# Adding products into spectral sums by accumulating DMAs from GpSimd, and one more down projection by seven products, in a two-layer convolution and FFN kernel

## The chip, the core and the metric

The kernel runs on one core of one Trainium2 chip. The metric is device time in microseconds, from the start to the end of the program. Five engines work side by side: TensorE (PE, matmuls), VectorE (DVE), ScalarE (ACT), GpSimd (POOL) and SyncE (SP, which issues most DMAs). They meet at semaphores alone. Sixteen DMA engines move the data that any of them orders.

## The reference

Sequence length S = 2048, width D = 512, inner width F = 1792, everything bfloat16 outside. Two rounds of the same two layers:

```python
def _A_ref(q, k, v, shift_k, ssm_k, ssm_D):
    # k_shift: causal convolution of k with 4 taps
    kv = k_shift * v
    # y: convolution along S of kv with ssm_k, by FFTs of length 2 S
    y = y + kv * ssm_D[None, None, :]
    return q * y

def _B_ref(x, w_gate, w_up, w_down):
    g = _silu(x @ w_gate)
    u = x @ w_up
    return (g * u) @ w_down

x = A_q
x = x + _A_ref(_layernorm(x, axis=-1), A_k, A_v, A_shift_k, A_ssm_k, A_ssm_D)
x = x + _B_ref(_layernorm(x, axis=-1), B_w_gate, B_w_up, B_w_down)
x = x + _A_ref(_layernorm(x, axis=-1), A_k, A_v, A_shift_k, A_ssm_k, A_ssm_D)
x = x + _B_ref(_layernorm(x, axis=-1), B_w_gate, B_w_up, B_w_down)
```

The long convolution y depends on k, v and ssm_k alone, so both rounds use the same y.

## The kernel before

The sequence is cut into 4 blocks of 512 tokens (index c or b). Each block of 512 rows is a tile of 128 partitions by 4 rows by 512 columns. A unit (layer, c, h) is half a block, 256 tokens, in one FFN layer: 16 units in all, run in the order (0,c,0), (0,c,1), (1,c,0), (1,c,1) for c = 0 to 3.

**The convolution by blocks.** Each block of kv and of ssm_k is turned into a spectrum by matmuls with a table of cosines and sines (`fwd`), evacuated by ACT, and combined by sums and differences on DVE (`butterfly4`). X[i] is the spectrum of block i of kv, G[j] that of a pair of neighbouring blocks of the kernel. Output block k needs the sum Z[k] of all products X[i] G[j] with i + j = k. `product` makes one: two multiplications of 128x4096 elements into t1 and t2 (L765), and two sums or differences of 128x2048 elements (L769). The first product of a sum writes Z itself. Each later one leaves its result in t1, and a DVE addition of 128x4096 elements adds t1 to Z (L773). There are six of these: one into Z[1], two into Z[2], three into Z[3]. `inverse` then folds Z by half sums and differences (m<-Z, L653), some more sums into Z (L659, L670) and goes back by matmuls with the table `inv` (ps<-Z,inv), which ACT evacuates into Yk.

**The FFN of a unit.** `prologue` normalises the rows, multiplies by y, adds to x, normalises again (the z rows, L976 on DVE or L971 on ACT), and turns z into zT by DMA transposes from SP (L1006); the first unit alone is turned by PE (ptz<-ident,z, L1034). The statistics come from DVE (`ln_stats`, BN_STATS L926 and BN_AGGR L927) or from ACT (`ln_stats_act`, L941 and L950), and the reciprocal square root (rstd) from a small operation on POOL (L912), for which the normalising instructions wait. The tables ST1 and ST2 say which units use ACT. Then come the gate and up projections in four groups of 4, 4, 4 and 2 tiles of 128 columns of F: either with the weights standing (`ffn`, L1256) or row by row (`by_rows`), where the products hr<-hr,sg (L1204, L1201) are turned back into sg by two DMA transposes from SP (L1206). The down projection reads them: 14 tiles times 2 row groups of matmuls with 512 columns (pd, L1287).

**Seven products.** For the units in STRASSEN the down projection of some or all groups is done by `seven`: a 2 by 2 blocking of tokens, tiles of F and columns of D, with seven products of 256 columns for a pair of tiles in place of eight. Its left sides are sums of the gated tiles, made by three DVE instructions a group (cb, L1076, L1078, L1080), its right sides five sums of w_down made once (`weight_sums`, L1061). `add_seven` evacuates four banks on ACT (mt, L1109) and merges them into x by five DVE instructions (L1114 to L1121). Without it two evacuations (dn) and one DVE addition (L1339) do this.

**What sets the order.** All instructions are recorded first, with their buffers. ORDER, a table of numbers, gives each recorded operation its place, and the engines' queues are filled in that order. The planner's `walk` goes through the order with cost constants, gives out the buffers of each ring (the ring "s8" has 11 slots for spectra, "ht" 7 for FFN tiles, "pf" 4 banks of PSUM), and sets where filler matmuls go at the start. Each engine works its queue strictly in order.

Of the kernel before, what the change touches and what calls it, by code (L numbers as in the profile page):

```python
# [9 lines left out]
P = 128  # L10
# [11 lines left out]
ST2 = lambda l, c, h: (l, c, h) in {(0, 0, 0), (0, 2, 1), (1, 2, 1)}  # L22
K_ACT = lambda b: b in {2, 3}
PW = 0.7
# [6 lines left out]
STRASSEN={(1,2,1):4,(0,3,0):4,(0,3,1):4,(1,3,0):4,(1,3,1):2}  # L31
# [125 lines left out]
class Plan:  # L157
# [15 lines left out]
    def add(self, eng, cost, emit, r=(), w=(), lat=None, due=None, conv=False, slack=0.0, after=(), dest=None):  # L173
# [22 lines left out]
        if o.late and any(q.eng == "ACT" for q in o.preds):  # L196
            o.late = 4
        if eng == "SP":
            o.late = 2 if cost == 1.29 else 3 if cost < 1 else 0
        o.count = 0  # L200
        if eng == "PE":
            o.count = 16
            for n in (512, 256, 128):
# [1402 lines left out]
```

## Time and profile before

| what | value |
| --- | --- |
| median of 3 runs | 338.25 us |
| lowest and highest run | 338.14 and 338.88 us |
| span of the profiled execution | 337.1 us |
| TensorE busy | 332.4 us, 2300 matmuls |
| VectorE busy | 314.3 us, 566 instructions |
| ScalarE busy | 269.4 us, 550 instructions |
| GpSimd busy | 36.1 us, 48 instructions |
| DMA, of all 16 engines' span | 38.3% in the queue of the kernel's own transfers |

The profile is of one execution; its own time is given as the span, from the first to the last instruction, and the runs' times lie about 1 us above it. Busy time of an engine counts instructions that overlap once. A matmul's end is modelled, so a busy TensorE may still have small holes between the starts of its matmuls. In a row of a group, the numbers behind the bar are the group's busy time and the mean of one instruction in ns, then the idle time just before them with what ended it. A row of the waits has the waiting instruction, what it waited for, the total in us, how many times, and the longest.

### The profile page before, as it was taken

How to read it: one execution, taken by the hardware profiler on the slowest of the kernel's cores; microseconds unless marked ns; L12 is line 12 of the kernel's file. 1: busy time of each engine (PE TensorE's matmuls, PEld its weight loads, DVE VectorE, ACT ScalarE, POOL GpSimd, SP SyncE). 2: the span in 40 equal slices, each digit the busy share in tenths (PEclk: the TensorE clock that was granted, in tenths of full speed). 3: DMA queues.
4: the chain of work that ended last, by engine and by line, in shares of the span. 5: the costliest groups of instructions: out<-in, count | busy, mean ns of one | idle time of the engine just before them, and what ended most of it. 6: DMA issues, size and time to landing. Idle time of an engine off the chain costs nothing.

```text
span 337.1 us, 6249 instructions
## 1 busy us (share of the span) xinstructions
PE 332.4 (99%) x2300; PEld 208.0 (62%) x2300; DVE 314.3 (93%) x566; ACT 269.4 (80%) x550; POOL 36.1 (11%) x48
## 2 busy tenths in 40 slices
PE   9999999999999999999999999999999999999996
PEld 7665865645445564644545474654445787878994
DVE  7799999999999999999999999997898998986995
ACT  6999999999966684989999794989765748476862
POOL 4010100031210100022110200021000000000000
PEclk9999999999999999999999999999999999999999
DMA  7999403632354446253314433320415320203001
GB/s 278 331 281 387 65 3 77 140 93 34 78 94 86 95 88 146 72 80 74 69 33 83 104 81 102 81 53 10 84 33 95 65 65 16 42 8 64 2 33 62
DMA packets 75817, 31.08 MB, mean 92 GB/s; under 512 B 67589, under 2 KB 73610, under 8 KB 75786
## 3 DMA queue, kind: packets, MB, share of 16 engines
q1 hardware_dynamic: 75632, 30.61, 38.3%
q8 instruction: 18, 0.29, 0.4%
q14 instruction: 13, 0.11, 0.1%
q10 hardware_dynamic: 154, 0.07, 0.1%
HBM read 12.33 MB, written 2.10 MB: 43 GB/s over the span
## 4 chain that ended last, share of the span: by engine, by line
PE 85%; DVE 10%; ACT 2%; issue 1%; POOL 0%; POOLq 0%
PE pf L423 48%; PE pd L1287 19%; PE ps L1097 7%; PE ps L423 6%; PE pf L1171 4%; DVE t L755 1%; PE wm L1572 1%; DVE Z L759 1%; DVE bst L926 1%; DVE t L769 1%; ACT jk L950 1%; DVE Z L773 1%; DVE t L765 1%; DVE m L896 1%; DVE z L976 1%
## 5 line engine op out<-in xcount | busy, mean ns | idle before, releaser
L423 PEld LDWEIGHTS <-zT 128*128 128x128 bf16 x496 | 48.5, 98 | 55.1 <-issue 0.2
L423 PE MATMUL pf<-wu_sb,zT 128*128 128x512 bf16 x248 | 61.5, 379 | 0.0
L423 PE MATMUL pf<-wg_sb,zT 128*128 128x512 bf16 x248 | 61.4, 379 | 0.0
L423 PE MATMUL pf<-zT,wg_sb 128*128 128x256 bf16 x400 | 50.7, 273 | 0.3 <-DVE zT L1037 0.3
L1197 ACT ACTIVATE sg<-pf 128x512 bf16<-128x512 f32 x62 | 37.4, 615 | 14.9 <-PE pf L423 10.7
L1287 PE MATMUL pd<-wd_sb,sg 128*128 128x512 bf16 x200 | 48.9, 379 | 0.0
L1198 ACT CAST hr<-pf 128x512 bf16<-128x512 f32 x62 | 36.3, 599 | 12.7 <-PE pf L423 10.9
L423 PEld LDWEIGHTS <-wg_sb 128*128 128x128 bf16 x400 | 38.6, 98 | 8.3 <-issue 0.7
L765 DVE TENSOR_TENSOR t<-X,G 128x4096 bf16<-128x4096 bf16 x18 | 41.0, 2287 | 0.1
L1258 ACT ACTIVATE sg<-pf 128x512 bf16<-128x512 f32 x50 | 29.6, 603 | 7.7 <-PE pf L423 6.3
L423 PE MATMUL pf<-zT,wu_sb 128*128 128x256 bf16 x272 | 34.9, 273 | 0.1
L912 POOL TENSOR_TENSOR rstd<-mv,nhalf 128x2 f32<-128x2 f32 x20 | 18.3, 919 | 147.8 <-DVE mv L927 147.8
L1287 PEld LDWEIGHTS <-sg 128*128 128x128 bf16 x200 | 19.6, 98 | 21.4
L423 PEld LDWEIGHTS <-wu_sb 128*128 128x128 bf16 x272 | 26.5, 98 | 6.6 <-issue 0.4
L1287 PE MATMUL pd<-wd_sb,ht 128*128 128x512 bf16 (+1 forms) x126 | 29.6, 369 | 0.0
L912 POOL TENSOR_TENSOR rstd<-ve,nhalf 128x2 f32<-128x2 f32 x12 | 13.8, 1150 | 119.6 <-ACT ve L954 119.6
L926 DVE BATCH_NORM_STATS2 bst<-xc 128x6 f32<-128x512 bf16 x40 | 26.3, 685 | 0.3
L1262 ACT CAST ht<-pf 128x512 bf16<-128x512 f32 x34 | 20.2, 599 | 1.6 <-PE pf L423 1.5
L1287 PEld LDWEIGHTS <-ht 128*128 128x128 bf16 x126 | 12.3, 98 | 13.4 <-DVE ht L1267 0.4
L532 ACT ACTIVATE X<-ps 128x512 bf16<-128x512 f32 x32 | 18.6, 606 | 2.3 <-PE ps L423 1.6
L1267 DVE TENSOR_TENSOR ht<-ht,sg 128x1024 bf16<-128x1024 bf16 (+1 forms) x33 | 18.3, 556 | 0.7 <-ACT sg L1258 0.4
L1204 DVE TENSOR_TENSOR hr<-hr,sg 128x1024 bf16<-128x1024 bf16 x25 | 17.1, 683 | 1.3 <-ACT sg L1197 0.9
(157 smaller groups left out, 590.9 us busy)
## 6 DMA issues: line engine op xcount, KB each, us to landing
hn<-in_A_ssm_k_dram SPq DMA_DIRECT2D x4, 512.0 KB, 4.0
vt<-in_A_v_dram SPq DMA_DIRECT2D x4, 512.0 KB, 6.0
xc<-in_A_q_dram SPq DMA_DIRECT2D x4, 512.0 KB, 5.3
out_dram<-xc SPq DMA_DIRECT2D x15, 128.0 KB, 1.9
wg_sb<-in_B_w_gate_dram SPq DMA_DIRECT2D x1, 1792.0 KB
wu_sb<-in_B_w_up_dram SPq DMA_DIRECT2D x1, 1792.0 KB, 7.6
wd_sb<-in_B_w_down_dram SPq DMA_DIRECT2D x1, 1280.0 KB, 11.5
sg<-hr SPq DMA_TRANSPOSE x62, 2.4
```

The lines of the kernel that those rows point to most:

```text
L423: nc.tensor.matmul(o, lhsT=lhsT, rhs=rhs, start=(n == 0), stop=(n == len(terms) - 1))
L532: add("ACT", act(D), lambda: nc.scalar.activation(out=view(), in_=ps.t[:], func=ACT.Copy, scale=scale), r=[ps], w=[(buf, keys)], conv=conv)
L765: dve(8 * D, lambda t=t, part=part: nc.vector.tensor_mul(out=t.t[:], in0=x.t[:, :, part:part + 1, :].to_broadcast((P, R, 2, D)), in1=g.t[: ...
L912: add("POOL", cost, lambda: nc.gpsimd.tensor_tensor(out=rstd.t[:], in0=var(), in1=nhalf.t[:].to_broadcast((P, n)), op=ALU.pow), r=reads + ...
L926: add("DVE", 0.6, lambda st=st, i=i: nc.vector.bn_stats(out=st.t[:, 0:6], in_=xs[c].t[:, i, :]), r=[(xs[c], (i,))], w=[st])
L1097: nc.tensor.matmul(bank.t[:, half_ * C:(half_ + 1) * C], lhsT=lhsT(i), rhs=rhs(i), start=(first and i == 0 and half_ == 0), stop=(last and ...
L1197: add("ACT", act(D), lambda ps=ps, dst=dst, o=o, which=which: nc.scalar.activation(out=rows(dst, o), in_=ps.t[:], func=ACT.Silu) if which ...
L1198: out=rows(dst, o), in_=ps.t[:], func=ACT.Silu) if which == "g" else nc.scalar.copy(out=rows(dst, o), in_=ps.t[:]),
L1258: add("ACT", act(D), lambda ps=ps, o=o, sg=sg: nc.scalar.activation(out=sg.t[:, o:o + 2, :], in_=ps.t[:], func=ACT.Silu), r=[ps], w=[(sg, ...
L1262: add("ACT", act(D), lambda ps=ps, o=o, ht=ht: nc.scalar.copy(out=ht.t[:, o:o + 2, :], in_=ps.t[:]), r=[ps], w=[(ht, (o // 2,))], due=(uni ...
L1267: dve(n * W, lambda sg=sg, ht=ht: nc.vector.tensor_mul(out=ht.t[:], in0=ht.t[:], in1=sg.t[:]), [sg], [ht], due=(unit, k / pairs, 0.0, "h"))
L1287: nc.tensor.matmul((pds[o] if not cs.start else pds[HP]).t[:, cs], lhsT=ht.tiles(q, o), rhs=wt["d"].t[:, ft, cs], start=(ft == std0 and no ...
```

## The change

Four things are changed.

1. The six additions of t1 to Z move from DVE to DMAs that add to their destination, issued by POOL (Z_DMA is true for all of them). DVE reads Z at m<-Z, so it has to wait for the last of these DMAs, and a DMA into a sum waits for the DMA before it into the same sum. The planner gets constants for them: 1.3 and 8.3 us, and no transposing DMA taken as landed within 9.4 us (plus 0.6) of such a start.
2. Unit (1,2,0) does its down projection by seven products in all four groups. So six units use them, and the sums of w_down are asked for one unit earlier.
3. The statistics of the second norm of unit (1,2,1) move from ACT to DVE (ST2).
4. The ring "jk" (scratch of ACT's statistics) gets two buffers, and fq, a table used at the start alone, takes a buffer of the ring "z".

ORDER is replaced as a whole, since the recorded operations are others.

```diff
-ST2 = lambda l, c, h: (l, c, h) in {(0, 0, 0), (0, 2, 1), (1, 2, 1)}
+ST2 = lambda l, c, h: (l, c, h) in {(0, 0, 0), (0, 2, 1)}
+Z_DMA = lambda i, j: True
-STRASSEN={(1,2,1):4,(0,3,0):4,(0,3,1):4,(1,3,0):4,(1,3,1):2}
+STRASSEN={(1,2,0):4,(1,2,1):4,(0,3,0):4,(0,3,1):4,(1,3,0):4,(1,3,1):2}
 ORDER = [
-    13, 127, 133, 202, 6, 0, 2, 4, 21, 5, 8, 1, 3, 9, 11, 17, 12, 18, 14, 19, 22, 20, 25, 24, 23, 26, 27, 37, 28, 31, 38, 69, 36, 60, 16, 52, 44,
...
+    1, 30, 38, 109, 3, 7, 10, 23, 20, 2, 4, 0, 5, 6, 8, 11, 12, 14, 13, 15, 21, 16, 19, 17, 18, 22, 27, 45, 28, 9, 101, 102, 41, 53, 54, 55,
...
+        if eng == "POOL" and lat is not None:
+            o.late = 5
...
+            if o.late == 5:
+                landed = max(landed, o.start + 9.4)
...
-    plan = Plan({"h": 1, "k": 1, "v": 1, "hs": 1, "dg": 1, "x": 2, "y": 2, "s8":11, "n": 2, "jk": 1, "dn": 1, "ks": 2, "z": 3, "zT":3,
+    plan = Plan({"h": 1, "k": 1, "v": 1, "hs": 1, "dg": 1, "x": 2, "y": 2, "s8":11, "n": 2, "jk": 2, "dn": 1, "ks": 2, "z": 3, "zT":3,
...
-    m4, fq = whole("m4", [P, R], F32), whole("fq", [P, P], F32)
+    m4, fq = whole("m4", [P, R], F32), new("z", "fq", [P, P], F32)
...
-        if not first:
+        if not first and Z_DMA(i, j):
+            add("POOL", 1.3, lambda: nc.gpsimd.dma_start(out=z.t[:], in_=t1.t[:], accum_op=ALU.add, max_dma_last_dim=4096), r=[t1], w=[z], lat=8.3, conv=conv)
+        elif not first:
             dve(8 * D, lambda: nc.vector.tensor_add(out=z.t[:], in0=z.t[:], in1=t1.t[:]), [t1], [z], conv=conv)
```

Line numbers of the changed kernel are 1 to 11 higher: L773 of before is L784 and no longer used, its DMA is L782, L653 is L662, L912 is L923, L1034 is L1045, L1204 is L1215.

On DVE, at the first addition into Z[1] (t_1096 is the product that is added, m<-Z the first reader of the sum), the order before is:

```order
L769 TENSOR_TENSOR t_1096<-t_1096,t_995 128x4x512 x2
L765 TENSOR_TENSOR t_1130<-X_640,G_703 128x4096
L773 TENSOR_TENSOR Z<-Z,t_1096 128x4096
L1339 TENSOR_TENSOR xc<-xc,dn 128x1024
L926 BN_STATS bst<-xc 128x6 x2
L927 BN_AGGR mv<-bst 128x2 x2
L653 TENSOR_TENSOR m<-Z 128x2048 x2
```

In the change the product is t_959. Its second half (L778) stands two rows ahead of these, with one BN_AGGR between, and the DMA on POOL can start from there:

```order
L774 TENSOR_TENSOR t_1123<-X_609,G_683 128x4096
L1350 TENSOR_TENSOR xc<-xc,dn 128x1024
L937 BN_STATS bst<-xc 128x6 x2
L938 BN_AGGR mv<-bst 128x2 x3
L987 TENSOR_SCALAR n<-xc,nm,rstd 128x512 x2
L987 TENSOR_SCALAR n<-xc,mv,rstd 128x512 x2
L1009 TENSOR_TENSOR n<-n,Yk 128x1024
L1010 TENSOR_TENSOR xc<-xc,n 128x1024
L1215 TENSOR_TENSOR hr<-hr,sg 128x1024
L937 BN_STATS bst<-xc 128x6 x2
L938 BN_AGGR mv<-bst 128x2 x2
L987 TENSOR_SCALAR n<-xc,mv,rstd 128x512
```

The next row is m<-Z (L662). The addition is gone, and eight rows of other work that stood behind m<-Z or elsewhere are put between the product and the reader.

On POOL, whose queue held only rstd in this part of the program, the DMAs stand among the rstd (t_1651 and t_1832 are the two products added to Z[2]):

```order
L782 DMA Z<-t_959 128x2x2048
L923 TENSOR_TENSOR rstd<-ve,nhalf 128x2
L923 TENSOR_TENSOR rstd<-mv,nhalf 128x2 x5
L782 DMA Z<-t_1651 128x2x2048
L782 DMA Z<-t_1832 128x2x2048
L923 TENSOR_TENSOR rstd<-ve,nhalf 128x2
L923 TENSOR_TENSOR rstd<-mv,nhalf 128x2
```

An rstd behind a DMA cannot be done before POOL has issued it, and the DMA of t_1832 waits until that of t_1651 has landed.

On PE, at the end of the start phase, the first unit's rows z are turned by matmuls (ptz). Before, the matmuls of the first inverse stand right ahead of them:

```order
L423 MATMUL ps<-dg,kTb 128x128
L902 LDWEIGHTS inv
L902 MATMUL ps<-m,inv 128x512
L902 LDWEIGHTS inv
L902 MATMUL ps<-m,inv 128x512
L902 LDWEIGHTS inv
L902 MATMUL ps<-m,inv 128x512
L1034 LDWEIGHTS z
L1034 MATMUL ptz<-ident,z 128x128
```

In the change:

```order
L432 MATMUL ps<-dg,kTb 128x128
L432 LDWEIGHTS fwd
L432 MATMUL ps<-vt,fwd 128x512
L1045 LDWEIGHTS z
L1045 MATMUL ptz<-ident,z 128x128
```

The inverse's matmuls have moved further ahead, and one matmul of the next block's spectrum (ps<-vt,fwd), which stood behind ptz, now stands ahead of it.

142 rows, old and new, of the table ORDER are left out of this document.

## The prediction

> **What bounds the kernel now.** I read the page's first part, then the engines by stretches of time, then PE's waits.
>
> ```profile
> span 337.1 us, 6249 instructions
> PE 332.4 (99%) x2300; PEld 208.0 (62%) x2300; DVE 314.3 (93%) x566; ACT 269.4 (80%) x550; POOL 36.1 (11%) x48
> ...
> 90.00:120.00 30.00, 30.00 (x159) 15.36 (x157) 29.52 (x43) 20.75 (x40) 2.47 (x2) 1.00 0.44 86
> ...
> 262.00:300.00 38.00, 38.00 (x373) 31.26 (x371) 35.24 (x99) 24.76 (x49) 2.09 (x3) 1.00 0.19 43
> ...
> 334.00:337.10 3.10, 0.00 (x0) 0.00 (x0) 0.19 (x1) 0.36 (x1) 0.00 (x0) 1.00 0.37 121
> ```
>
> In the stretches the columns behind the length are busy time of PE, PEld, DVE, ACT and POOL, then the granted clock. PE is busy all the time at the full clock, but VectorE (DVE) is close behind it: 29.52 of 30 us between 90 and 120 us. Busy matmuls can hide small holes, so the waits come next.
>
> ```profile
> PE wm L1572 <- PEq L1590: 0.8, 1, 0.8
> PE ptz L1034 <- DVE z L976: 0.3, 1, 0.3
> PE pf L423 <- DVE zT L1037: 0.3, 1, 0.3
> ```
>
> These are all of PE's recorded waits: 1.4 us, all in the first 33.1 us. So PE's stream of matmuls is the bound, with DVE feeding it just in time. The time can fall only by PE work removed and by the few holes filled; it can rise by any wait that the new transfers put on PE.
>
> **The change, part by part.** *Down projection of unit (1,2,0) by seven products.* PE's pitch comes from long pieces of the chain, one of each kind:
>
> ```profile
> 48.50 4.32 PE pd L1287 x20
> ...
> 326.54 4.69 PE ps L1097 x43
> ```
>
> A 512-column matmul costs 4.32 / 20 = 0.216 us, a 256-column one 4.69 / 43 = 0.109 us. The unit's 14 tiles times 2 row groups are 28 matmuls, 28 x 0.216 = 6.05 us. Seven products of half the width for each of 7 pairs of tiles are 49 matmuls, 49 x 0.109 = 5.34 us. PE gains **0.71 us**, and since PE is the bound this goes straight into the time, if it stays fed.
>
> *PE's order at the start.* One more 512-column matmul (ps<-vt,fwd) now stands ahead of the first transposes ptz.
>
> ```profile
> 30.56 0.81 PE L902 MATMUL ps<-m,inv 128*128 128x512 bf16 x3
> 31.68 0.72 PE L1034 MATMUL ptz<-ident,z 128*128 128x128 bf16 x8 [0.31 <-DVE z L976]
> ```
>
> Three matmuls from 30.56 on are issued by 31.21; the next starts at 31.68, a hole of 0.47 us in which PE waits for z. DVE's order up to z differs only in the arrangement of the same products, so z should come when it came. The extra matmul fills 0.216 us of the hole and is missing later: **-0.22 us** (between 0, if z is later by as much, and -0.22).
>
> *Six additions taken off DVE, and what DVE gets.*
>
> ```profile
> L765 DVE TENSOR_TENSOR t<-X,G 128x4096 bf16<-128x4096 bf16 x18 | 41.0, 2287 | 0.1
> L926 DVE BATCH_NORM_STATS2 bst<-xc 128x6 f32<-128x512 bf16 x40 | 26.3, 685 | 0.3
> L1204 DVE TENSOR_TENSOR hr<-hr,sg 128x1024 bf16<-128x1024 bf16 x25 | 17.1, 683 | 1.3 <-ACT sg L1197 0.9 <-ACT hr L1198 0.4
> L773 DVE TENSOR_TENSOR Z<-Z,t 128x4096 bf16<-128x4096 bf16 x6 | 13.7, 2287 | 0.0
> L1339 DVE TENSOR_TENSOR xc<-xc,dn 128x1024 bf16<-128x1024 bf16 x11 | 7.5, 684 | 0.0
> L927 DVE BATCH_NORM_AGGREGATE mv<-bst 128x2 f32<-128x9 f32 x40 | 6.3, 182 | 0.2
> L976 DVE TENSOR_SCALAR n<-xc,nm,rstd 128x512 bf16<-128x512 bf16 x10 | 3.9, 408 | 2.0 <-POOL rstd L912 2.0
> L1114 DVE TENSOR_TENSOR xc<-xc,mt 128x1024 bf16<-128x1024 bf16 x5 | 3.4, 688 | 1.3 <-ACT mt L1109 1.3
> L1076 DVE TENSOR_TENSOR cb<-sg 128x512 bf16<-128x512 bf16 x6 | 2.5, 414 | 0.2 <-issue 0.2
> L1078 DVE TENSOR_TENSOR cb<-sg 128x512 bf16<-128x512 bf16 x6 | 2.5, 413 | 0.0
> L1116 DVE TENSOR_TENSOR xc<-xc,mt 128x512 bf16<-128x512 bf16 x5 | 2.1, 422 | 0.2
> L1080 DVE TENSOR_TENSOR cb<-sg 128x256 bf16<-128x256 bf16 x6 | 1.7, 285 | 0.0
> ```
>
> Off: 6 x 2.29 = 13.7 us (L773). On: three full groups of sums, 3 x (0.414 + 0.413 + 0.285) = 3.3, and a half group, at most 2 x 0.285 + 0.285 = 0.9; the merge, 0.688 + 4 x 0.422 = 2.4, less the one L1339, 0.7; and the statistics of (1,2,1), which leave ACT, 2 x (0.685 + 0.182) = 1.7. Net 13.7 - 3.3 - 0.9 - 2.4 + 0.7 - 1.7 = 6.1 us less DVE work. All of it lies beside PE; I price it at **0**. It is room against late transfers. ACT loses the four passes over rows of these statistics and gets two more evacuations; at 80% busy it is not the bound. The five sums of wd that the unit's seven products read keep their number and only have to be done one unit earlier; fq in a z buffer is read long before the first z is written, and a second jk buffer only takes a wait of ACT for itself away: all at 0, hidden behind PE's matmuls, and the whole of it bounded by the room that DVE gains, 6.1 us.
>
> *Six accumulating transfers.* The trace has none, so I bound one from both sides. It carries 1 MB, and must read the destination as well.
>
> ```profile
> hn<-in_A_ssm_k_dram SPq DMA_DIRECT2D x4, 512.0 KB, 4.0
> ...
> wu_sb<-in_B_w_up_dram SPq DMA_DIRECT2D x1, 1792.0 KB, 7.6
> ...
> sg<-hr SPq DMA_TRANSPOSE x62, 2.4
> ```
>
> Low: 1 MB at the rate of the load of wu, 7.6 / 1.75 = 4.3 us. High: 2 MB read at the rate of hn, 4 x 4.0 = 16 us. I take 2 MB at wu's rate, 8.7 us, since the size is nearest to that row, and 1 us for POOL's issue (between 0 and 2.2, below): 9.7 us from the product's end to the sum. The planner's own allowances are no measurement and are not used.
>
> By the Trainium skill ("DMA: Bandwidth & Descriptors", the anatomy of one DMA on the gpsimd path) a DMA takes some 2.0 us and its bytes at 436 GB/s, which gives an estimate of 4.4 us here; this trace's wu took 7.6 where the same rule gives 6.2, so the sum would keep its zero below and gain margin.
>
> What covers it is DVE's work up to the first reader, the half sums m<-Z. For the first transfer that is 20 instructions (the order of DVE above shows nearly all of them): one of 4096 elements, 2.29 us; four of 1024, 2.7; four BN_STATS, 2.7; six BN_AGGR, 1.1; five TENSOR_SCALAR, 2.0; 10.9 us by the means. Neighbours overlap:
>
> ```profile
> 62.60 0.68 DVE L1204 TENSOR_TENSOR hr<-hr,sg 128x1024 bf16<-128x1024 bf16 x1
> 63.20 1.28 DVE L926 BATCH_NORM_STATS2 bst<-xc 128x6 f32<-128x512 bf16 x2
> ```
>
> The next starts 0.60 us after one of 0.68, so each of the 20 gives back 0.08: 10.9 - 1.6 = **9.3 us** of cover. Counted alike, the third transfer has 9.8 us and the sixth 10.5; the second, fourth and fifth have 14 us or more up to the next transfer into the same sum, which POOL holds back until the one before has landed. So at 9.7 us DVE waits 0.4 us once, and POOL never; behind POOL's issues stand only the rstd of later norms. Whether PE sees it is read at the old place:
>
> ```profile
> 87.06 0.68 DVE L659 TENSOR_TENSOR Z<-m 128x1024 bf16<-128x1024 bf16 x1
> ...
> 89.86 1.03 PE L423 MATMUL ps<-Z,inv 128*128 128x512 bf16 x4
> ```
>
> DVE's last write of Z ends at 87.74 and PE's second group of inverse matmuls starts at 89.86: 2.1 us of room at the tightest of the three. The transfers therefore cost **0** up to about 9.3 + 2.1 = 11.4 us.
>
> Sum: -0.71 - 0.22 = -0.93 us on the profiled span of 337.1 us, 336.2. The profile gives that execution's span alone; the median of the runs, 338.25, lies 1.15 us above it, and I carry this over: **337.3 us**.
>
> **Rivals.** *The transfers are slow (slower).* Place: the three reads m<-Z. It decides from 11.4 us on. Halfway between 8.7 and 16, at 12.4 us and 1 for the issue, they are 4.1, 3.6 and 2.9 us late; less 2.1 us of room PE loses 2.0, 1.5 and 0.8, and the time is 337.3 + 4.3 = **341.6 us**. Against it speaks the 6.1 us of DVE work gone, most of it ahead of the third read. Chance 0.14.
>
> *The transposing DMAs stand still behind the transfers (slower).* SP issues them in order, and beside loads they slow down:
>
> ```profile
> 26.88 8.45 SPq L467 DMA_TRANSPOSE kTb<-in_A_k_dram  x1
> ...
> 149.28 3.15 SPq L467 DMA_TRANSPOSE kTb<-in_A_k_dram  x1
> ...
> ACT sg L1197 <- DMA sg<-hr: 2.8, 1, 2.8
> ```
>
> The same transpose holds SP 8.45 us beside loads and 3.15 without. The order shows that only the first transfer's stretch is nearly free of them: behind the second an hr product, whose transposes follow, ends within 1 us, behind the fourth likewise, behind the third and sixth after some 4 us. If such a pair lands up to 8.45 - 3.15 = 5.3 us late, ACT waits for the sg buffer as it once does now (2.8 us), and then PE for ACT. With PE losing 1 us at two of the four places the time is **339.3 us**. For it: the flights overlap in order; against: the sg tiles are made several groups ahead. Chance 0.14.
>
> *POOL is held by DVE, and the transfers start late (no change).*
>
> ```profile
> 46.51 0.69 POOL L912 TENSOR_TENSOR rstd<-mv,nhalf 128x2 f32<-128x2 f32 x1 [8.22 <-DVE mv L927]
> ...
> 72.85 2.86 POOL L912 TENSOR_TENSOR rstd<-ve,nhalf 128x2 f32<-128x2 f32 x1 [7.29 <-ACT ve L954]
> ```
>
> The same small POOL operation takes 0.69 us, or 2.86 beside DVE's long products: 2.2 us of being held. Behind the first transfer's issue a 4096-element product follows on DVE. Held alike, the sum is there after 11.9 us, 2.6 late, and PE loses 2.6 - 2.1 = 0.5; the rstd queued behind the issue on POOL is late too and the normalised rows n wait for it, which trace L976 shows as 2.0 us now, so another 0.3 us or so: **338.1 us**. Chance 0.20, with any other small giving back of the gain.
>
> The Trainium skill ("SBUF — State Buffer", the two separate sides and who interferes with whom) warns of hiding such a DMA under DVE work, since descriptors can't be written while DVE works in a two-port mode, but says that tensor_tensor holds only GpSimd's reads. The held rstd agrees with the second half; by it the large products would not delay the issue, the 0.4 us TENSOR_SCALARs would, and this rival would shrink to the forecast.
>
> *More is gained.* PE also has a hole of 0.33 us that no wait shows:
>
> ```profile
> 259.12 0.38 PE L1097 MATMUL ps<-wsa,sg 128*128 128x256 bf16 x2
> 259.45 0.39 PE L1097 MATMUL ps<-wsb,sg 128*128 128x256 bf16 x2
> 259.68 1.26 PE L1097 MATMUL ps<-wd_sb,cb 128*128 128x256 bf16 x8
> 260.78 1.03 PE L423 MATMUL pf<-wg_sb,zT 128*128 128x512 bf16 x4
> ```
>
> Two matmuls take 0.33 where 0.22 is their pitch, and eight 1.10 where it is 0.87: 0.11 + 0.23 of waiting for DVE's sums cb. With DVE freed ahead, the hole goes: **337.0 us**; the rest of the start's holes too, 336.4. Chance 0.17, with the forecast's own 0.35.
>
> **How the numbers follow.** Forecast 337.3 with 0.35, 337.0 with 0.17, no change 0.20, the two slower rivals 0.14 each. 0.2%, about what a measurement of this kernel tells from no change, is 0.68 us: faster means under 337.57, slower over 338.93. Faster 0.52, same 0.20, slower 0.28. The range goes from 336.4 to 341.0; about 0.12 lies above it (most of the first rival), and little below.
>
> **What would show it.** Right: 2321 matmuls; PE's waits still about 1 us, none behind 33 us; DVE busy about 308 us; m<-Z without a wait, or one below 2 us. The accumulating DMAs' time to landing decides: up to 10 us supports the forecast, over 11.4 the first rival. Transposes sg<-hr landing far over 2.4 us beside them, with ACT waiting for sg, show the second; an rstd or an issue of over 2 us on POOL the third. Wrong altogether would be a hole at ptz larger than 0.47 us, or PE waiting for cb in unit (1,2,0), whose sums now come earlier.

## The result, and the profile after

| | before | after |
| --- | --- | --- |
| median of the runs | 338.37 us (338.14 to 338.88, 4 runs: the three of the table above and one more) | 349.75 us (349.56 to 350.08, 4 runs) |
| ratio | | 1.0334, 95% interval 1.0320 to 1.0349 |
| span of the profiled execution | 337.1 us | 347.8 us |

The change makes the kernel 11.4 us slower; the prediction was 337.3 us in a range of 336.4 to 341.0. Here and in the experiments the time lies about 1.8 us above the span, so the span of 337.1 us belongs to the run of 338.88 us, half a microsecond above the median; the spans therefore differ by less than the medians. One execution of e7_copy, an experiment below, and the only one of it that was profiled, took 435.93 us at a mean granted clock of 0.755, so it is left out of that experiment's time and nothing is read from its profile. The page of the changed kernel begins so, and its chain of work that ended last is shared out so by engine:

```profile
span 347.8 us, 6307 instructions
...
PE 333.5 (96%) x2321; PEld 209.5 (60%) x2321; DVE 310.0 (89%) x580; ACT 267.9 (77%) x542; POOL 37.6 (11%) x54
...
PE 51%; DVE 23%; DMA 10%; ACT 7%; SPq 4%; issue 2%; POOL 1%; DVEq 0%; ACTq 0%; POOLq 0%
```

PE has the 2321 matmuls that were foreseen and is busy for 96% where it was 99%. DVE has been relieved and is less busy, but the last chain now runs through DVE, DMAs and SP's queue. PE's waits say where:

```profile
PE pd L1298 <- DMA sg<-hr: 5.5, 3, 3.2
PE ps L432 <- DVE vt L738: 3.2, 1, 3.2
PE wm L1583 <- PEq L1601: 0.8, 1, 0.8
PE ps L432 <- ACT ks L636: 0.5, 1, 0.5
```

The first is a wait for the transposing DMAs that turn the gated rows: 3.2 us at 129 us, 1.6 us at 231 us, and 0.7 us at 115 us, where no transfer flies. The second waits for DVE, and DVE in turn for another transposing DMA, as the waits of the other engines show:

```profile
DVE vt L738 <- DMA kc<-ka: 5.5, 1, 5.5
ACT ht L1273 <- DMA sg<-hr: 5.4, 2, 3.9
```

In the chain that ended last, the transpose that DVE waits for lands 8.50 us after its issue:

```profile
197.58 8.50 DMA kc<-ka
```

The same execution in stretches (columns as in the prediction's first view) shows where PE's time is lost:

```profile
112.00:120.00 8.00, 7.31 (x43) 3.93 (x42) 7.97 (x8) 4.22 (x8) 0.00 (x0) 1.00 0.53 109
120.00:146.00 26.00, 22.81 (x119) 11.87 (x118) 19.27 (x27) 15.03 (x34) 3.14 (x3) 0.93 0.89 173
146.00:200.00 54.00, 53.77 (x293) 28.41 (x292) 51.86 (x82) 50.46 (x101) 7.71 (x8) 1.00 0.36 73
200.00:208.00 8.00, 4.80 (x27) 2.33 (x25) 2.52 (x5) 2.44 (x5) 0.00 (x0) 1.00 0.88 140
208.00:229.00 21.00, 20.70 (x125) 11.91 (x124) 20.25 (x26) 17.68 (x43) 2.93 (x3) 1.00 0.61 116
229.00:240.00 11.00, 9.40 (x53) 4.89 (x51) 9.83 (x15) 4.83 (x10) 1.12 (x2) 1.00 0.50 70
```

PE's idle time, the stretch less the first busy number, is 0.7, 3.2, 0.2, 3.2, 0.3 and 1.6 us, in all 9.2. In the second stretch the granted clock is 0.93 on the mean. A finer cut finds why:

```profile
129.10:132.50 3.40, 0.37 (x2) 0.00 (x0) 1.80 (x1) 0.00 (x0) 0.00 (x0) 1.00 1.30 157
132.50:133.86 1.36, 1.20 (x6) 0.60 (x7) 0.53 (x2) 0.71 (x2) 0.00 (x0) 1.00 0.56 139
133.86:137.20 3.34, 3.34 (x10) 1.21 (x8) 3.31 (x3) 0.96 (x2) 0.00 (x0) 0.50 0.82 308
```

After the wait PE starts at 132.66 us at the full clock, and 1.2 us later it works at half the clock for 3.34 us, which costs another 1.7 us. Over the whole span PE's idle time grows from 337.1 - 332.4 = 4.7 to 347.8 - 333.5 = 14.3 us, and its busy time by 1.1 us, about the 1.7 of the half clock less the 0.7 that the seven products save. 9.6 + 1.1 = 10.7 us is the whole difference of the spans.

And the transfers? Their landing, from issue to the end, and the landing of the sg transposes issued between 120 and 131 us, beside the second transfer:

```profile
Z<-t POOLq DMA_DIRECT2D x6, 1024.0 KB, 8.3
...
DMA to landing us min/median/max: 3.3/7.0/10.1
```

A transfer takes 8.3 us (7.9 to 9.3), and no engine waits for a sum: m<-Z is in no list of waits. A transpose takes 7.0 instead of the 2.4 of before. The DMA queues from 120 to 131 us (packets, MB, share of 16 engines):

```profile
q1 hardware_dynamic: 3374, 0.94, 61.1%
q0 software_dynamic: 272, 1.05, 56.9%
```

The first is that of the kernel's own transfers, the second that of the accumulating ones. Together they have 118%, more time in flight than the 16 engines have, so the packets of both are in flight on the same engines at the same time.

### The profile page after: what moved, and what is told of

It reads as the page before. It is cut to its first block, busy times and chain, and to the rows that moved or that the text cites. A ratio compares the mean times of both kernels' runs of the same rounds, so it can differ in the third digit from the quotient of the medians.

```text
span 347.8 us, 6307 instructions
## 1 busy us (share of the span) xinstructions
PE 333.5 (96%) x2321; PEld 209.5 (60%) x2321; DVE 310.0 (89%) x580; ACT 267.9 (77%) x542; POOL 37.6 (11%) x54
## 4 chain that ended last, share of the span: by engine, by line
PE 51%; DVE 23%; DMA 10%; ACT 7%; SPq 4%; issue 2%; POOL 1%; DVEq 0%; ACTq 0%; POOLq 0%
PE pf L432 28%; PE ps L1108 9%; PE pd L1298 8%; DMA sg<-hr 5%; PE pf L1182 4%; DVE t L774 3%; PE ps L432 3%; DMA kc<-ka 2%; DVE bst L937 2%; DVE m L662 2%; SPq L717 1%; DVE t L764 1%; DMA kn<-in_A_k_dram 1%; ACT jk L961 1%; DVE ht L1278 1%
## 5 line engine op out<-in xcount | busy, mean ns | idle before, releaser
L432 PE MATMUL pf<-wu_sb,zT 128*128 128x512 bf16 x248 | 62.3, 379 | 0.2 <-DMA zT<-z 0.2
L1298 PE MATMUL pd<-wd_sb,sg 128*128 128x512 bf16 x176 | 43.9, 384 | 5.6 <-DMA sg<-hr 5.5
L1298 PEld LDWEIGHTS <-sg 128*128 128x128 bf16 x176 | 17.0, 98 | 25.9 <-DMA sg<-hr 7.3
L923 POOL TENSOR_TENSOR rstd<-mv,nhalf 128x2 f32<-128x2 f32 x21 | 17.6, 845 | 132.0 <-DVE mv L938 132.0
L937 DVE BATCH_NORM_STATS2 bst<-xc 128x6 f32<-128x512 bf16 x42 | 27.4, 682 | 0.3
L1108 PEld LDWEIGHTS <-cb 128*128 128x128 bf16 x195 | 19.0, 98 | 2.9
L1120 ACT CAST mt<-ps 128x512 bf16<-128x512 f32 (+1 forms) x24 | 12.6, 535 | 9.7 <-PE ps L1108 9.6
```

The lines of the kernel that those rows point to most:

```text
L432: nc.tensor.matmul(o, lhsT=lhsT, rhs=rhs, start=(n == 0), stop=(n == len(terms) - 1))
L923: add("POOL", cost, lambda: nc.gpsimd.tensor_tensor(out=rstd.t[:], in0=var(), in1=nhalf.t[:].to_broadcast((P, n)), op=ALU.pow), r=reads + ...
L937: add("DVE", 0.6, lambda st=st, i=i: nc.vector.bn_stats(out=st.t[:, 0:6], in_=xs[c].t[:, i, :]), r=[(xs[c], (i,))], w=[st])
L1108: nc.tensor.matmul(bank.t[:, half_ * C:(half_ + 1) * C], lhsT=lhsT(i), rhs=rhs(i), start=(first and i == 0 and half_ == 0), stop=(last and ...
L1298: nc.tensor.matmul((pds[o] if not cs.start else pds[HP]).t[:, cs], lhsT=ht.tiles(q, o), rhs=wt["d"].t[:, ft, cs], start=(ft == std0 and no ...
```

## The experiments

Every time is a median in us, beside runs of the kernel before on the same chip (338.23 to 338.43). First theory: transposing DMAs are late beside a transfer, and that alone is the loss. Rival: the new order itself, or its DVE or POOL queue, is late.

**The additions back on DVE, all or some; order as in the change.** The three values of Z_DMA are those of e1_dve, of e2_136 (first, third and sixth by transfers) and of e3_245 (second, fourth and fifth), in this order.

```diff
-Z_DMA = lambda i, j: True
+Z_DMA = lambda i, j: False
+Z_DMA = lambda i, j: (i, j) in {(1, 0), (2, 0), (3, 0)}
+Z_DMA = lambda i, j: (i, j) in {(0, 2), (2, 1), (0, 3)}
```

> The changed kernel with all six additions back on DVE; order, seven products and everything else as in the change. Theory (transposing DMAs that fly beside an accumulating one land 4 to 8 us late and PE waits for them): PE's waits at 129, 203 and 231 us are gone, with the stretch at half clock behind the first of them; DVE has 13.7 us more to do in an order not made for it, so 337.5 to 340 us. Rival (the new order or the seven products themselves cost the time): 345 us or more.

> Accumulating DMAs for the first, third and sixth addition alone, beside which the profile of the change shows transposes landing in about 2.4 us; the other three on DVE. Theory: no wait of PE for a transpose over 1 us, 337 to 339 us. Rival (any accumulating DMA costs, by DVE waiting for the sum or POOL being held): 341 to 345 us, about half of the loss.

> Accumulating DMAs for the second, fourth and fifth addition alone; the other three on DVE. Theory: the same waits of PE as in the change, behind sg and kc transposes, 347 to 351 us. Rival (all six share the loss): 342 to 345 us.

Measured: e1_dve 348.89 (ratio 1.0306, interval 1.0288 to 1.0323), e2_136 348.81 (1.0295, 1.0272 to 1.0317), e3_245 354.83 (1.0491, 1.0472 to 1.0511). Without any transfer the changed order is nearly as slow as with all six, and with DVE's additions and the three flights it is slowest. For e1_dve the rival's 345 us or more came out, for another reason than the rival gave, as is seen below; e2_136 and e3_245 are slower than both sides of their expectations. PE's waits in e1_dve are others, though:

```profile
PE pd L1298 <- DMA sg<-hr: 2.9, 3, 1.2
PE pf L432 <- ACT hr L1209: 2.6, 1, 2.6
PE pd L1298 <- DVE ht L1278: 1.2, 1, 1.2
```

ACT itself waits 4.1 us for a sum of rows xc from DVE in this run. DVE's timeline of e1_dve (start, length) shows the place:

```profile
214.74 1.22 DVE L778 TENSOR_TENSOR t<-t,t 128x2048 bf16<-128x2048 bf16 x1
215.88 4.61 DVE L784 TENSOR_TENSOR Z<-Z,t 128x4096 bf16<-128x4096 bf16 x2
...
222.28 0.68 DVE L1350 TENSOR_TENSOR xc<-xc,dn 128x1024 bf16<-128x1024 bf16 x1
```

Two additions stand back to back, 4.6 us, ahead of the xc that ACT wants. The change's order spends the time that the additions leave free, so undoing the transfers alone tells nothing of them: it puts 13.7 us of DVE work back where no room is left. Between experiment and theory stood a second effect, and the next kernels take it out.

**The fourth transfer ahead of the rstd.** POOL issues it 11.6 us after its product is ready (184.65 us, DVE), since an rstd that waits for ACT stands in front of it:

```profile
195.37 0.89 POOL L923 TENSOR_TENSOR rstd<-ve,nhalf 128x2 f32<-128x2 f32 x1 [26.42 <-ACT ve L965]
196.21 1.22 POOL L782 DMA_DIRECT2D Z<-t  x1
```

```diff
+        table = list(ORDER)
+        fourth = [o for o in plan.ops if o.eng == "POOL" and o.lat is not None][3]
+        table[fourth.n] = max(table[q.n] for q, data in fourth.preds.items() if data) + 0.5
-        plan.issue(*plan.order(ORDER), 6.0, warm)
+        plan.issue(*plan.order(table), 6.0, warm)
```

> The fourth accumulating DMA stands ahead of an rstd in POOL's queue, so that it starts when its product is done (184.7 us) and not behind that rstd (196.2 us). Theory: it no longer flies beside the kc transposes, and PE's 3.2 us wait for vt at 203 us goes; it now flies beside four sg transposes at 186 to 192 us, whose tiles may be late in place of it: 345.5 to 348 us. Rival (the place of the fourth does not matter): 349.7 us.

Measured: 350.90 (1.0365, 1.0350 to 1.0381), a microsecond slower than the change, where 345.5 to 348 was expected. The transfer starts at 184.87, and the wait for vt at 203 us is gone; in its place PE waits 4.9 us for sg at 189 us, the longest of three in

```profile
PE pd L1298 <- DMA sg<-hr: 8.8, 3, 4.9
```

At either place there are transposes beside it, and one that PE waits for is late.

**Neither transfers nor additions.** Each addition is cut to 64 of 4096 columns, so the sums lack the later products almost everywhere; all else stays. Once in the change's order, once in the order before.

```diff
-            dve(8 * D, lambda: nc.vector.tensor_add(out=z.t[:], in0=z.t[:], in1=t1.t[:]), [t1], [z], conv=conv)
+            dve(64, lambda: nc.vector.tensor_add(out=z.t[:, 0, 0, 0:64], in0=z.t[:, 0, 0, 0:64], in1=t1.t[:, 0, 0, 0:64]), [t1], [z], conv=conv)
```

> The changed kernel with neither transfers nor full additions: each of the six additions is a DVE one over 64 columns, so the spectral sums keep their first product alone almost everywhere, and the order of all operations stays that of the change. Theory (the time is lost where transposing DMAs fly beside an accumulating one; without the transfers the same order waits only because DVE has 13.7 us of additions more): both costs are gone, so the time is the prediction's sum, 337.3 us (336.5 to 338.5), with PE's waits under 2 us in all. Rival A (the new order itself is late somewhere, with or without transfers): 340 us or more with waits of PE for ht, hr or sg that stand at the same places as with the additions on DVE. Rival B (the slower sevenths of unit (1,2,0) cost): waits for cb near 255 us and some 339 us.

> The kernel before, with its six additions cut to 64 columns each (the sums keep their first product almost everywhere), its order unchanged: what DVE's 13.7 us alone are worth. If PE's matmuls are the bound, as the prediction read: 338.0 to 338.4 us, at most 0.4 us faster (the hole at the sums cb). Rival (PE's stream is fed so late by DVE that freeing DVE shortens it): 336 us or less.

Measured: e5_none 338.32 (0.9998, 0.9986 to 1.0009), e6_bnone 338.52 (1.0005, 0.9995 to 1.0014), beside 338.28; the second is 0.1 us above its range, less than the noise. In e5_none the sg transposes of 120 to 131 us land after 2.4, and PE's only waits are these:

```profile
PE wm L1583 <- PEq L1601: 0.8, 1, 0.8
PE pf L432 <- DMA zT<-z: 0.6, 1, 0.6
PE ps L432 <- ACT ks L636: 0.5, 1, 0.5
PE ps L432 <- DVE hs L615: 0.3, 1, 0.3
PE pd L1298 <- DMA sg<-hr: 0.2, 1, 0.2
```

So the change's order with additions on DVE costs 10.6 us over the same order without them, and with the transfers 11.4: in this order the six additions are dear wherever they are done, and two different causes give like times. The order alone is not late. But it gives no gain either: e5_none is 1.0 us above the predicted sum. And 13.7 us less of DVE work bring the kernel before nothing, as PE's bound says.

**Which transfers cost.** Like e5_none, but with three of the six transfers: e10_245n has the second, fourth and fifth, e11_136n the others.

```diff
+Z_DMA = lambda i, j: (i, j) in {(0, 2), (2, 1), (0, 3)}
+Z_DMA = lambda i, j: (i, j) in {(1, 0), (2, 0), (3, 0)}
```

> The changed kernel with transfers for the second, fourth and fifth products alone; the additions of the first, third and sixth are cut to 64 columns on DVE, so those products are left out of the sums almost everywhere. DVE thus has no additions to make and flies only the three transfers that stand beside transposes. If these three carry the whole loss: 347 to 350 us, with PE's waits near 129, 203 and 230 us as in the changed kernel. If the loss is spread over all six: half, near 344 us.

> The changed kernel with transfers for the first, third and sixth products alone; the additions of the second, fourth and fifth are cut to 64 columns on DVE, so those products are left out of the sums almost everywhere. Before each of these three readings of the sum DVE waits for the landing, if it comes late. If transfers without transposes beside them are free, as the prediction priced them: 338.0 to 339.0 us, as without any transfer and addition (338.3). If the three readings wait, or the loss is spread over all six: 340 us or more, with waits of DVE for the transfer.

Measured: e10_245n 349.56 (1.0344, 1.0321 to 1.0367), e11_136n 341.75 (1.0114, 1.0071 to 1.0157). PE's waits in e10_245n, then in e11_136n:

```profile
PE pd L1298 <- DMA sg<-hr: 5.4, 2, 3.8
PE ps L432 <- DVE vt L738: 3.4, 1, 3.4
```

```profile
PE pd L1298 <- DMA sg<-hr: 2.3, 2, 2.1
```

The second, fourth and fifth alone bring the whole loss: DVE has no full addition to make there, and the time is that of the change. The other three, which I had expected to be free, are not (3.4 us), and the two losses do not add up to that of the change: the third now flies from 136.17 on, because PE has not lost 3 us before it, and meets the sg transposes from 139.9 on, which land after up to 5.4 us. In the change it starts at 138.65 and PE is later by its losses; there the two sg transposes that follow land after 2.5. DVE waits for none of the sums here either.

**What makes the transposes late: bytes, pieces or the adding?** The transfers without the adding (the sum keeps its last product alone), and with the rows cut finer. The first edit is e7_copy, and made to e10_245n it is e12_245c; the second is e8_small.

```diff
-accum_op=ALU.add, max_dma_last_dim=4096
+max_dma_last_dim=4096
...
-accum_op=ALU.add, max_dma_last_dim=4096
+accum_op=ALU.add, max_dma_last_dim=512
```

> The changed kernel with its six transfers as plain copies of the product over the sum (the sum keeps its last product alone): the same bytes written, nothing added, the same places. If the accumulation makes the transfers long and the transposes late: landing about 5 us or less in place of 8.3, transposes beside them under 4 us, and 338 to 342 us. If any transfer of 1 MB in 4 KB pieces does it: landing near 8 us, transposes of the pairs behind the second near 7 us, and 348 to 350 us.

> The changed kernel with the rows of its accumulating transfers cut into pieces of 512 elements (1 KB in place of 4 KB). If a transpose is late because its small pieces queue behind the long pieces of the transfer (0.36 us each): transposes beside them land in 3 to 5 us and the time falls to 340 to 345 us, unless POOL's issue, now with four times the pieces, grows beyond 3 us. If they share the bandwidth or something else by bytes: landing 6.7 us or more as before and 348 us or more. If the issue grows fourfold (5 us) and the landing too, the sums come late: waits at m<-Z and over 350 us.

> The kernel with transfers for the second, fourth and fifth products alone, as plain copies of the product over the sum in place of additions (those sums lose what was in them; the additions of the first, third and sixth are cut to 64 columns on DVE). Beside it stands the same kernel with adding transfers, 349.56 us. If the adding makes the transfers hold the DMA engines (6.1 us each, against 2.8 for a copy) and so the transposes beside them: transposes behind the second land in 2.5 to 4 us, PE's waits near 129, 203 and 230 us shrink to under 1 us each, and the time is 338.3 to 340 us. If any transfer of 1 MB beside them does it: waits of 2 us and more at these places and 343 us or more.

Measured: e7_copy 340.57 (1.0067, 1.0044 to 1.0091; four runs); e8_small 363.48 (1.0755, 1.0722 to 1.0787); e12_245c 340.60 (1.0064, 1.0047 to 1.0080) where the same three transfers with the adding took 349.56. The page's line of the transfers' queue (packets, MB, share of 16 engines) and their landing, after the change, in e12_245c and in e8_small:

```profile
q0 software_dynamic: 1632, 6.29, 10.5%
...
Z<-t POOLq DMA_DIRECT2D x6, 1024.0 KB, 8.3
```

```profile
q0 software_dynamic: 816, 3.15, 2.6%
...
Z<-t POOLq DMA_DIRECT2D x3, 1024.0 KB, 5.5
```

```profile
q0 software_dynamic: 12384, 6.29, 16.1%
...
Z<-t POOLq DMA_DIRECT2D x6, 1024.0 KB, 12.3
```

One adding transfer holds each DMA engine for 0.105 x 347.8 / 6 = 6.1 us, one copy for 0.026 x 339.6 / 3 = 2.9, one adding transfer in eight times as many pieces (of about 0.5 KB, not the 1 KB that I expected) for 0.161 x 363.7 / 6 = 9.8. Transposes of 120 to 131 us land after 7.0, 4.8 and 7.1 us. PE's waits in e12_245c:

```profile
PE pd L1298 <- DMA sg<-hr: 1.3, 4, 0.5
PE pf L432 <- DMA zT<-z: 0.9, 2, 0.5
...
PE ps L432 <- DVE vt L738: 0.3, 1, 0.3
```

No wait above 0.5 us is left at the three places. So it is the adding that costs, not the megabyte, and shorter pieces make it worse. That it costs by the time for which it holds the DMA engines fits the three times above. This time isn't a wait for other packets: from 239 to 249 us in the change the adding queue has 61.1% of 10 us beside 13.3% of the kernel's own queue, and a copy in e12_245c from 213 to 223 us has 27.7% beside 13.0%. Transposes beside the copies landed later than expected, after 4.8 us against 2.5 to 4, and the time is 0.6 us above the range: 1 MB of copy beside transposes isn't free either. In e8_small DVE also waits for a sum, 2.6 us once.

**Flights put behind the transposes.** Ahead of the fourth and the fifth transfer POOL multiplies two columns of a tile that a transposing DMA writes, so that the flight starts when this one has landed. (The second stays where it is, since the third product takes the buffer of the second's in the ring "s8".)

```diff
+            def go():
+                e = dst.t[:, o, 0, 0:2] if dst.name == "sg" else dst.t[:, 0, o, 0:2]
+                nc.gpsimd.tensor_tensor(out=gate[:], in0=e, in1=e, op=ALU.mult)
+                emit()
...
+            flight.preds[turn] = True
+            table[flight.n] = max(table[flight.n], table[turn.n] + 0.5)
```

> The changed kernel, its fourth and fifth transfers held back: ahead of each POOL multiplies two columns of a tile that a transposing DMA has written (the pair issued near 203 us, the one near 224 us), so that the transfer starts when that transpose has landed, in a stretch without others. The second can't be held back so: the third product takes the buffer of the second's (11 slots in the ring). If a transfer costs by the transposes that fly beside it: the waits near 203 us (3.3) and 230 us (1.8) go, the one near 129 us (3.4, then half clock) stays, and the time is 343.5 to 346 us. If these waits come from DVE or the order and not from the overlap: 348 us or more. If the later landing holds DVE up (the buffers of the products come free later): DVE waits of several us for POOL's transfers, and no gain either.

Measured: 352.03 (1.0403, 1.0374 to 1.0431). The waits at 203 and 230 us are gone, as the theory says, but the time is worse than in the change. The third expectation, DVE late and no gain, comes nearest, though DVE waits for an rstd here and not for a buffer. POOL and PE:

```profile
232.96 1.21 POOL L782 DMA_DIRECT2D Z<-t  x1
241.45 1.20 POOL L782 DMA_DIRECT2D Z<-t  x1 [7.27 <-DMA Z<-t]
242.20 1.19 POOL L923 TENSOR_TENSOR rstd<-ve,nhalf 128x2 f32<-128x2 f32 x1
```

```profile
PE ps L1108 <- DMA sg<-hr: 6.2, 1, 6.2
PE pd L1298 <- DMA sg<-hr: 3.8, 2, 3.5
```

The fifth flight ends at 240.9, the sixth has to wait for it (same sum), and the rstd queued behind the sixth is late. DVE waits 6.7 us for it with n, so hr and xc follow late, and then the sg transposes fly beside the sixth transfer: the last chain has 4.82 us for the one that PE waits for. A free stretch for one flight took it away from the next.

No kernel here is faster than the one before: even with transfers and additions at no price, in e5_none, the change's order only equals it. An order made anew for either side was not tried.

## Why the prediction was wrong, point by point

- *PE's stream is the bound, and DVE's relief is worth nothing by itself.* Right: e6_bnone, 338.52 beside 338.28.
- *Seven products of unit (1,2,0), -0.71 us.* The count holds: by the records 28 matmuls of 512 columns have gone and 49 of 256 have come. But e5_none shows no net gain, so something in the new order takes it back. Besides wm, PE waits 0.6 + 0.5 + 0.3 + 0.2 = 1.6 us there and 0.3 + 0.3 = 0.6 before: 1.0 us more, as much as is missing from the predicted sum. These are one execution of each kernel, and that the waits are the whole difference wasn't tested.
- *The start, -0.22 us.* It came out near 0, the end of its range: ptz now starts without a wait, but the extra matmul in front of it waits 0.51 us for ACT (ks), and 0.09 us are lost ahead of pf, where PE had waited 0.31 for z and 0.26 for zT. A matmul put into a hole has its own operand to wait for.
- *DVE at about 308 us.* 310.0, which is 4.3 us less than before and not 6.1.
- *A transfer takes 8.7 us to land and POOL 1 us to issue.* The sizes are right: 8.3 (7.9 to 9.3) and 1.20 to 1.38 us. The 8.7 was 2 MB at the rate of a load, picked out of 4.3 to 16 us; no run shows that the second read is what makes an adding transfer long, so the hit is partly luck. *The sums are read without a wait.* Right as well, in the change and in both halves of it, and so the first rival fell. By the Trainium skill ("DMA: Bandwidth & Descriptors", the anatomy of one DMA on the gpsimd path) the estimate was 4.4 us; the plain copy of the same megabyte is nearer to it, 5.5 us (5.2 to 6.2) in e12_245c, than the adding one. The page gives no price for the adding.
- *"The transfers therefore cost 0 up to about 11.4 us."* **This is the step that failed.** It asked only who reads the sum. It left out who else uses the 16 DMA engines while the transfer flies: the transposes, which PE needs a few microseconds later. The same page of the Trainium skill says it plainly (section of the rules for kernel authors: DMAs issued from SP, ACT and GpSimd run on the same 16 engines and interleave), and the trace agrees with shares of 61.1% and 56.9% in one stretch.
- *The second rival, transposes that stand still.* The mechanism was this one, at 0.14, and its sign came: ACT waits 5.4 us for sg. Its price of 2 us for two of four places was the mis-sized term: PE lost 3.2 + 1.7, 3.2 and 1.6 us at three. The bound that I had worked out for a late pair, 5.3 us, was near what was measured (7.0 - 2.4 = 4.6 at the median, 10.1 - 2.4 = 7.7 at most). I discounted it by "the sg tiles are made several groups ahead", which I had not read from any row. e10_245n and e12_245c show it: the same transfers cost 11.2 us over e5_none with the adding and 2.3 without.
- *The fourth as I placed it.* I looked for what stands behind a transfer in POOL's queue, not for what stands in front. An rstd with 26 us of waiting for ACT does, and it moves the flight 11.6 us on, onto the kc transposes. e4_pool shows that this place is not what costs: without it the time is 350.90.
- *POOL held by DVE's long products.* Fell: no issue took over 1.4 us.
- *Undoing the transfers would give back the old time.* Not written in the prediction, but my first theory assumed it, and e1_dve refuted it: an order that has been made for a relief depends on it.

## What to carry to other kernels

Work moved from a busy engine to DMAs is not moved to an idle place: count, for the time of its flight, every other transfer that needs the DMA engines and how soon its reader wants it, and price a transfer by the engine time that its queue's line shows, not by when its own result is read. An accumulating transfer is dear in that currency: twice a copy here. When the change comes with a new order, cut the suspected work out of both orders (as e5_none and e6_bnone do) before you undo it in one, since putting it back measures the order as much as the work.

## What the runs showed of the hardware that I had not expected

- An adding transfer of 1 MB within the on-chip memory lands after 8.3 us and holds each DMA engine for 6.1, a copy 5.5 and 2.9; pieces of 0.5 KB make the adding one 12.3 and 9.8, and POOL's issue 2.1 us at the median instead of 1.2.
- Beside an adding transfer not only the landing of a transpose grows (2.4 to 7.0 us) but SP's time to issue it too: 1.19 us each in e5_none, up to 3.09 after the change.
- After PE's wait of 3.2 us at 129 us the granted clock was 0.50 for 3.3 us, beginning 1.2 us after PE had resumed; after a wait just as long at 203 us it stayed at 1.00. The Trainium skill ("TensorE: Matmul & The Clock Gate", part 1 on the clock gate) puts the limit for idle time at about 3.4 us, in windows that run freely. The other runs do not fit such a limit: in e1_dve the clock was 0.50 from 225.2 to 228.6 us after a wait of 2.58 us, and in e3_245 it stayed at 1.00 after one of 3.65 us at 131 us. So the length of the wait alone does not decide; what does stays open here.
